# Shifted values copied by engines instead of by DMA, together with a new plan and new buffer counts, in an attention and feed-forward kernel

## The chip, the cores and the metric

The kernel runs on one core of a Trainium2 chip. The metric is the device time in microseconds of one execution. A kernel is executed several times beside the kernel before on the same chip; each execution is called fast or slow, and only fast ones are compared. Of every kernel one execution was also profiled. In the profiles the span (first to last instruction) is 1.7 us shorter than the device time of the same execution (271.4 and 273.11 before), and the last matmul starts 3.0 to 3.1 us before the span ends. That is why the text can speak of "the start of the last matmul" as the end of the work.

## The reference, cut to what matters

Four batches of 768 tokens, 8 heads of 64 features. Three heads use full causal attention, five see 4 sink tokens and a window of 64. The 3072 x 512 result goes through a gated feed-forward layer.

```python
scores = scale * q @ k.T                    # causal; five heads masked to sink + window
a = softmax(scores); x = (a @ v)            # -> 3072 x 512
g = x @ w_gate                              # 512 -> 1536
ffn_out = (gelu(g) * (x @ w_val)) @ w_out   # 1536 -> 512
return x + sigmoid(x @ w_res) * ffn_out
```

## The kernel before

The program is not written in the order in which it runs. It is a graph of tasks (an engine, an assumed duration, the tasks it depends on, a priority, its buffers), and a list scheduler walks through assumed time and fixes each engine's order before anything is compiled. A DMA's assumed landing gets an extra allowance, `late`. `HINTS` overrides priorities by task number. The numbers are guesses that shape the order; on the chip each instruction simply waits for what it depends on, in the order that was fixed.

```python
# inside the scheduler: when a DMA is thought to have landed
st = max(now + dur + 0.8, dma_free[e])
both = min(t.dma, max(0.0, dma_free[other] - st))
dma_free[e] = st + t.dma + both
...                                             # the other queue is pushed back by `both`
t.end = dma_free[e] + 1.6 + t.late
```

The window attention needs the values `va` shifted by half a tile. That shifted copy is `vs`. For the first chunk, tile 1 is copied by VectorE or ScalarE; tiles 2 and 3 go by two DMA transfers from SyncE's queue as long as `VS_DMA` is 1:

```python
for lo, hi, pr in ((1, 2, -75),) + (() if VS_DMA else ((2, 4, 130),)):
    for dst, src, off in ((0, 64, 1), (64, 0, 0)):
        ... e.activation(...) if on == "act" else e.tensor_copy(out=o, in_=i_)   # 64 x (hi-lo)*520
if not VS_DMA:
    return
...                                             # the two transfers, on SyncE:
ts.append(G.add("sp", 1.2, ... e.dma_start(vs[dst:dst + 64, ...], va[src:src + 64, ...])))
```

All weights come through GpSimd's queue, alternately a block of the gate (`wg`) and of the value weights (`wv`), three of each, 512 KB apiece. The attention output of a chunk is normalised, transposed to `xT` and multiplied with these blocks. The first chunk has its `xT` from TensorE, in two halves of 256 columns; for the third chunk half of `xT` comes by a DMA transpose on SyncE's queue:

```python
t = G.add("sp", 1.3, ... e.dma_start(xT[:, cb:cb + 2, :], x16, transpose=True), ..., name="xD")
t.late = 4.0
...
# first chunk: 4 matmuls of 256 columns per weight tile and half
tt = [G.add("pe", ..., xT half deps + [wtok[nm, f // 4]]) for nm, w, dst in (("g", wg, gb), ("v", wv, vb))]
# other chunks and the later part of the first: 512 columns, first cb 0 and 1, then cb 2 and 3
```

While TensorE waits for its first data it runs fillers, 128-column matmuls on a tile of zeros called `blank`; after the weights are there no filler runs.

The softmax here doesn't subtract the row's maximum and nothing guards it: scores larger than these inputs give would overflow.

Of the kernel before, what the change touches and what calls it, by code (L numbers as in the profile page):

```python
# [10 lines left out]
D_MODEL = NHEAD * DHEAD  # L11
# [3 lines left out]
NCB = D_MODEL // 128  # L15
# [3 lines left out]
FP16 = mybir.dt.float16  # L19
FP32 = mybir.dt.float32  # L20
# [23 lines left out]


HINTS = (
    "3:-32.45 398:-150.8 399:-169.97 400:-169.2 401:-150.79 406:481.05 428:533.75 430:564.21 587:-160.89 "
    "608:614.87 617:480.76 622:-210.99 632:614.85 641:12.83 691:-144.85 692:87.22 699:675.15 702:-204.03 "
    "703:-258.78 709:-3118.71 710:-58.5 711:-96.86 715:37.85 723:2455.64 726:495.66 727:-164.98 738:-53.4 "
    "739:-73.39 740:-45.28 746:978.76 747:1556.14 750:37.86 756:509.01 766:947.54 773:2472.11 800:2517.53 "  # L50
    "822:510.02 904:2457.97 910:1055.17 929:2531.59 934:2383.41 959:3505.35 960:1941.27 999:2033.43 "
    "1004:2019.58 1016:3479.78 1061:3558.68 1066:1999 1091:2536 1093:2446.41 1104:4380.53 1107:1523.27 "
    "1109:2000.01 1113:3498.6 1125:4512.49 1136:4434.23 1142:4479.26 1147:4467.42 1152:4500.85 1228:0.01 "
    "1230:3502.12 1236:3515.97 1247:2929.46 1249:3037.51 1258:3472.01 1273:4410.03 1277:0 1278:4479.25 "
    "1304:5410.01 1333:4393.08 1335:5399.49 1338:4000.81 1339:4038.38 1340:4017.53 1347:3851.4 1445:4017.95 "
    "1446:4523.33 1451:3511 1469:6427.61 1479:4849.77 1481:5510 1485:5546.83 1486:6329.91 1490:6560.66 "
    "1501:5520.23 1503:5026.6 1504:5301.09 1539:5026.6 1552:6385.88 1654:4896.34 1675:7440.39 "
)

class Task:  # L60
# [115 lines left out]
SWITCH = 0.1  # L176
SWAP = -3000.0
VK_AT = -18.5
VS_DMA = 1
LAT = {"pe": 0.20, "act": 0.10, "dve": 0.08, "pool": 0.12, "sp": 0.1}  # L180


# [274 lines left out]
def build_kernel(nc, q, k, v, w_gate, w_val, w_out, w_res, out):  # L457
# [3 lines left out]
    many = lambda name, n, shape, dt: [sb(f"{name}{i}", shape, dt) for i in range(n)]  # L461
# [16 lines left out]
    P_er = Pool(many("er", 2, [128, 4608], FP16))  # L478
    P_es = Pool(many("es", 2, [128, 1024], FP16))
    P_ek = Pool(many("ek", 1, [128, 640], FP16))  # L480
    P_x = Pool(many("xtok", 3, [128, 4, D_MODEL], FP32))
    P_x16 = Pool(many("x16", 2, [128, 2, 4, 128], FP16))
    P_xt = Pool(many("xT", 3, [128, NCB, 512], FP16))
    P_h = Pool(many("hT", 2, [128, NF, 512], FP16))
    P_ga = Pool(many("gact", 3, [128, 512], FP16))
    P_sr = Pool(many("srs", 2, [128, 512], FP32))
    P_ot = Pool(many("otile", 3, [128, D_MODEL], FP32))
    P_rc = Pool(many("rcp", 3, [128, 2, 4], FP32))
    psum = nc.alloc_psum_tensor("ps", [128, 8 * 512], FP32)
    one = lambda *bs: [(b,) for b in bs]  # L490
# [6 lines left out]
    def at(buf):  # L497
        if buf.pool is P_ps:
            return psum[:, buf.slot[0] * 512:(buf.slot[-1] + 1) * 512]
        return buf.pool.items[buf.slot]  # L500
# [46 lines left out]
    def dma(eng, prio, cost, out_ap, in_ap, bufs=(), deps=(), name="ld", grp=None):  # L547
        issue = 0.85 if eng == "pool" else 1.2
        return G.add(eng, issue, lambda e: e.dma_start(out_ap(), in_ap), deps, prio, bufs=bufs, dma=cost, name=name, grp=grp)  # L549

    wtok = {}

    def load_weights():
        for j in range(3):
            for nm, t, src in (("g", wg, w_gate), ("v", wv, w_val)):
                s = slice(j * 512, (j + 1) * 512)
                wtok[nm, j] = dma("pool", -20 + j, 2.6, (lambda t=t, s=s: lambda: t[:, :, s])(),
                                  src[:, s].rearrange("(ci p) f -> p ci f", p=128))
        wtok["r"] = dma("pool", -12, 2.6, lambda: wr[:, :, :], w_res.rearrange("(ci p) f -> p ci f", p=128))
        for j in range(4):  # L560
            s = slice(j * 3, (j + 1) * 3)
            wtok["o", j] = dma("pool", -11 + j, 1.95, (lambda s=s: lambda: wo[:, s, :])(),
                               w_out[j * 384:(j + 1) * 384, :].rearrange("(fi p) c -> p fi c", p=128))
            wtok["o", j].late = 2.2

    class B:
        pass
# [12 lines left out]
    def values(b, a, z, base, each, on_engines=False):  # L580
# [23 lines left out]
        if on_engines:  # L604
            ts = []
            for lo, hi, pr in ((1, 2, -75),) + (() if VS_DMA else ((2, 4, 130),)):
                for dst, src, off in ((0, 64, 1), (64, 0, 0)):
# [11 lines left out]
            late_copies.extend(ts)  # L619
            if not VS_DMA:  # L620
                return
# [93 lines left out]
    def ph(c, part):  # L715
        return phase.setdefault((c, part), [])

    def attention(c, segs, xbuf, xtbuf, xtoks, xttoks, l0=0, last=(), ek=None):
# [46 lines left out]
        for P in todo:  # L765
            if P.heads[0] % 2 == 0:
                x16 = Buf(P_x16)
                xdeps = []
            last, tn = weigh(P, tiles, sinks, xbuf, x16, xtoks, xdeps, last, l0)
            if P.heads[0] % 2 == 1:  # L770
                if c >= DT_FIRST and P.p == order[1]:
                    to_features_dma(c, P.heads[0] // 2, P.pr, x16, xdeps, xtbuf, xttoks)
                else:
                  for cb in (P.heads[0] // 2, P.heads[1] // 2):
                    to_features(c, cb, P.pr, x16, xdeps, xtbuf, xttoks, l0, len(tiles))
                if P is todo[-1]:
                    tn.order += [t for _, t in xttoks[-2:]]
                if c == 0 and P is todo[-1]:
                    for t in norms[1:]:
                        t.order.append(xdeps[-1])  # L780
            norms.append(tn)
# [234 lines left out]
    def to_features_dma(c, cb, pr, x16, xdeps, xtbuf, xttoks):  # L1016
        t = G.add("sp", 1.3, lambda e: e.dma_start(
            at(xtbuf)[:, cb:cb + 2, :].rearrange("p c (i k) -> p (c i) k", k=128), at(x16)[:, :, :, :].rearrange("p c i k -> p (c i k)"), transpose=True),
            xdeps, pr - 4003, bufs=[x16, xtbuf], dma=1.2, name="xD")
        t.late = 4.0  # L1020
        ph(c, "xT").append(t)
        xttoks += [(cb, t), (cb + 1, t)]

# [108 lines left out]
    for _ in range(360):  # L1132
# [3 lines left out]
    G.add("act", 0.2, lambda e: e.activation(out=scratch[:, :], in_=blank[:, 0:1], func=AF.Exp), [t_blank], -99,  # L1136
          fset="exp", name="table")
    load_weights()
    for c, segs in enumerate(CHUNKS):
        lt0 = 0  # L1140
# [19 lines left out]
    for c in range(len(CHUNKS)):  # L1160
        gv, gelu = ph(c, "gv"), ph(c, "gelu")
# [23 lines left out]
def bass_duo_attention_split__then__geglu_gated_residual_kernel(  # L1185
    nc: bass.Bass,
    q: bass.AP,
    k: bass.AP,
    v: bass.AP,
    is_retrieval: bass.AP,  # L1190
    n_sink: bass.AP,
    window: bass.AP,
    moe_w_gate: bass.AP,
    moe_w_val: bass.AP,
    moe_w_out: bass.AP,
    moe_w_res: bass.AP,
    out: bass.AP,
):
    assert int(n_sink) == N_SINK and int(window) == WINDOW
    build_kernel(nc, q, k, v, moe_w_gate, moe_w_val, moe_w_out, moe_w_res, out)  # L1200
# [33 lines left out]
```

## Time and profile before

| | before |
|---|---|
| median of the first runs | 273.0 us |
| span of the profiled run | 271.4 us |
| first matmul with weights starts | 20.40 us |
| last matmul starts | 268.33 us |
| TensorE busy | 98% |

Between the two starts lie 247.93 us in which TensorE does almost nothing but follow one matmul with the next. The page's row of shares along the chain of waits says the same: almost all of the end hangs on TensorE itself, and a small part on DMA.

```profile
PE 88%; DMA 6%; DVE 1%; POOL 0%; issue 0%; DVEq 0%
```

In the timelines (start, duration, engine, line, operation; in brackets the idle time before it and what ended that) the last eviction of the first half's `xT` on ScalarE, which frees the weight matmuls, starts at 18.59 and takes 0.38 us, after 0.50 us of idle time.

```profile
8.72 0.64 PE L668 MATMUL ps<-ident,qks 128*64 128x128 f16 x16
...
18.59 0.38 ACT L1033 ACTIVATE xT<-ps 128x256 f16<-128x256 f16 x1 [0.50 <-PE ps L1026]
```

The last `xT` is ready at 18.97, but the value weights land at 20.35: the start is bound by that transfer.

### The profile page before, as it was taken

Reading aid. Unit: us, or ns where it says so; the run is one execution under the profiler, and the core shown is the slowest. Engines: PE = TensorE matmul, PEld = TensorE weight load, DVE = VectorE, ACT = ScalarE, POOL = GpSimd, SP = SyncE. Lnnn points to the kernel's source line nnn. Section 1 sums busy time; section 2 is a strip of 40 time slices with the busy share of each in tenths; the row PEclk is TensorE's granted clock in tenths of the full one; section 3 lists DMA queues with packets and bytes.
Section 4 is the critical chain, followed back from the end, with each engine's and each line's share of the span. In section 5 each row is a group of like instructions: output and inputs, shape, how many; then the busy total and the mean of one; then the engine's idle time right before and its main releaser. Section 6 shows DMA issues by size and latency. Waiting matters only on the chain.

```text
span 271.4 us, 5681 instructions
## 1 busy us (share of the span) xinstructions
PE 265.2 (98%) x2394; PEld 138.8 (51%) x2394; DVE 140.5 (52%) x272; ACT 139.9 (52%) x214; POOL 87.0 (32%) x124
## 2 busy tenths in 40 slices
PE   7989999999999999999999999999999999999995
PEld 7767654455444456344445444455444355444444
DVE  2795354388442567444377354476543457544344
ACT  3784457784435876224764324776332878233210
POOL 8999419995535039990000000000000000000000
PEclk9999999999999999999999999999999999999999
DMA  6999999999999999999954100013100014200013
GB/s 85 172 217 207 188 176 229 173 161 176 189 154 151 154 172 178 179 198 143 139 134 116 42 0 0 2 41 97 61 0 0 0 41 80 77 2 1 0 39 118
DMA packets 97002, 29.13 MB, mean 107 GB/s; under 512 B 85456, under 2 KB 93264, under 8 KB 96976
## 3 DMA queue, kind: packets, MB, share of 16 engines
q0 software_dynamic: 70320, 14.69, 64.7%
q1 hardware_dynamic: 26656, 14.07, 27.1%
q8 instruction: 19, 0.31, 0.5%
q14 instruction: 7, 0.06, 0.1%
HBM read 29.36 MB, written 6.29 MB: 131 GB/s over the span
## 4 chain that ended last, share of the span: by engine, by line
PE 88%; DMA 6%; DVE 1%; POOL 0%; issue 0%; DVEq 0%
PE ps L1072 43%; PE ps L1117 22%; PE ps L1102 7%; PE ps L813 5%; DMA wv<-in_moe_w_val_dram 3%; DMA xT<-x 3%; PE ps L1054 3%; PE ps L947 3%; PE ps L937 2%; PE ps L961 1%; PE ps L1026 1%; PE ps L668 1%; PE ps L904 1%; DVE otile L1124 0%; DVE otile L1121 0%; POOL wg L549 0%
## 5 line engine op out<-in xcount | busy, mean ns | idle before, releaser
L1086 DVE SCALAR_TENSOR_TENSOR hT<-gact,ps 128x512 f16<-128x512 f16 x68 | 45.8, 686 | 67.5 <-ACT gact L1084 38.7
L1084 ACT ACTIVATE gact<-ps 128x512 f16<-128x512 f32 x68 | 40.1, 597 | 74.2 <-PE ps L1072 71.2
L1072 PE MATMUL ps<-xT,wg 128*128 128x512 f16 x272 | 74.7, 379 | 0.6 <-DMA xT<-x 0.6
L1072 PE MATMUL ps<-xT,wv 128*128 128x512 f16 x272 | 74.2, 379 | 0.0
L1117 PE MATMUL ps<-wo,hT 128*128 128x512 f16 (+2 forms) x312 | 70.0, 363 | 0.0
L1072 PEld LDWEIGHTS ps<-xT,wv 128*128 128x128 f16 x272 | 26.3, 98 | 31.8 <-issue 0.7
L1072 PEld LDWEIGHTS ps<-xT,wg 128*128 128x128 f16 x272 | 26.3, 98 | 31.6 <-DMA xT<-x 1.1
L1117 PEld LDWEIGHTS ps<-wo,hT 128*128 128x128 f16 x312 | 27.2, 98 | 26.5 <-issue 0.6
L549 POOL DMA_DIRECT2D qks<-in_k_dram x36 | 28.9, 850 | 31.3 <-DMA qkt<-qks 21.7
L829 ACT ACTIVATE er<-ps 128x1024 f16<-128x1024 f32 (+4 forms) x40 | 34.2, 891 | 9.2 <-PE ps L813 8.8
L549 POOL DMA_DIRECT2D qks<-in_q_dram x36 | 29.2, 863 | 0.8 <-POOLq L1216 0.8
L1102 PE MATMUL ps<-wr,xT 128*128 128x512 f16 x96 | 24.5, 379 | 0.0
L1121 DVE SCALAR_TENSOR_TENSOR otile<-srs,ps 128x512 f32<-128x512 f32 (+2 forms) x26 | 16.7, 643 | 14.6 <-PE ps L1117 12.2
L549 POOL DMA_DIRECT2D va<-in_v_dram x24 | 21.5, 958 | 2.7 <-PE ps L961 2.7
L1105 ACT ACTIVATE srs<-ps 128x512 f32<-128x512 f32 x24 | 14.3, 596 | 12.8 <-PE ps L1102 12.5
L813 PE MATMUL ps<-qkt 64*128 64x64 f16 (+3 forms) x399 | 17.9, 215 | 0.0
L1124 DVE TENSOR_TENSOR otile<-otile,xtok 128x512 f32<-128x512 f32 (+2 forms) x26 | 16.8, 648 | 0.8
L1004 DVE TENSOR_TENSOR xtok<-ps,rcp 128x512 f32<-128x512 f32 (+1 forms) x28 | 17.0, 609 | 0.3
L813 PEld LDWEIGHTS ps<-qkt 64*128 64x128 f16 x399 | 10.3, 94 | 9.2 <-issue 3.8
L1102 PEld LDWEIGHTS ps<-wr,xT 128*128 128x128 f16 x96 | 8.7, 98 | 10.0 <-issue 0.8
L829 ACT ACTIVATE es<-ps 128x1024 f16<-128x1024 f32 (+1 forms) x14 | 12.6, 898 | 1.3 <-PE ps L813 1.1
L1134 PE MATMUL ps<-blank 128*128 128x128 f16 x119 | 11.5, 246 | 1.1 <-DVE blank L521 1.1
(67 smaller groups left out, 208.9 us busy)
## 6 DMA issues: line engine op xcount, KB each, us to landing
out_dram<-otile SPq DMA_DIRECT2D x23, 256.0 KB, 2.0
va<-in_v_dram POOLq DMA_DIRECT2D x24, 128.0 KB, 18.0
qks<-in_k_dram POOLq DMA_DIRECT2D x32, 64.0 KB, 13.7
qks<-in_q_dram POOLq DMA_DIRECT2D x32, 64.0 KB, 13.6
wg<-in_moe_w_gate_dram POOLq DMA_DIRECT2D x3, 512.0 KB, 11.0
wv<-in_moe_w_val_dram POOLq DMA_DIRECT2D x3, 512.0 KB, 11.4
wo<-in_moe_w_out_dram POOLq DMA_DIRECT2D x4, 384.0 KB, 23.5
vs<-va SPq DMA_DIRECT2D x4, 260.0 KB, 5.7
```

The costliest lines, as they stand in the source:

```text
L549: return G.add(eng, issue, lambda e: e.dma_start(out_ap(), in_ap), deps, prio, bufs=bufs, dma=cost, name=name, grp=grp)
L813: return [e.matmul(at(scr)[:, oo:oo + w], lhsT=at(BB.qkt)[half, 1, p, k0:k0 + 128], rhs=at(BB.qkt)[half, 0, p, qq:qq + w], start=True, sto ...
L829: return e.activation(out=o, in_=i_, func=AF.Exp, scale=SM_SCALE)
L1004: t2 = G.add("dve", c_dve(2 * n * 64), lambda e: e.tensor_tensor(out=xview(), in0=avv(0, DHEAD), in1=scale(), op=ALU.mult), [t1] + xdeps, ...
L1072: return lambda e: [e.matmul(at(dst)[:, :], lhsT=w[:, ci, f * 128:(f + 1) * 128], rhs=at(xtbuf)[:, ci, :], start=(ci == 0), stop=(ci == NC ...
L1084: ta = G.add("act", c_act(512), (lambda gb=gb, ga=ga: lambda e: e.activation(out=at(ga)[:, :], in_=at(gb)[:, :], func=AF.Gelu))(), [tg], p ...
L1086: th = G.add("dve", c_dve(512), (lambda vb=vb, ga=ga, f=f: lambda e: e.scalar_tensor_tensor(out=at(h)[:, f, :], in0=at(ga)[:, :], scalar=0 ...
L1102: e.matmul(at(rb)[:, :], lhsT=at(xtbuf)[:, ci, s], rhs=wr[:, ci, :], start=(ci == 0), stop=(ci == NCB - 1))
L1105: ta = G.add("act", c_act(512), (lambda rb=rb, sr=sr: lambda e: e.activation(out=at(sr)[:, :], in_=at(rb)[:, :], func=AF.Tanh, scale=0.5)) ...
L1117: e.matmul(at(fb)[:, w], lhsT=at(h)[:, fi, s], rhs=wo[:, fi, w], start=(fi == 0), stop=(fi == NF - 1))
L1121: t1 = G.add("dve", c_dve(n), (lambda fb=fb, sr=sr, ot=ot, w=w: lambda e: e.scalar_tensor_tensor(out=at(ot)[:, w], in0=at(sr)[:, w], scala ...
L1124: t2 = G.add("dve", c_dve(n), (lambda ot=ot, lt=lt, w=w: lambda e: e.tensor_tensor(out=at(ot)[:, w], in0=at(ot)[:, w], in1=at(xbuf)[:, lt, ...
```

## The change

Its intent: take 0.27 MB of copying off the DMA queues while the weights are loading, let the plan know that one transpose lands later than it thought, and shift buffers from `x` and `xT` to gelu results and output tiles. The priorities were tuned anew for it, so the orders change in many places. `HINTS` is cut here: 24 lines of numbers, all different.

```diff
-    "3:-32.45 398:-150.8 399:-169.97 ... 1675:7440.39 "
+    "0:39.65 1:493.12 14:469.96 398:-242.8 ... ~632:477.39 ~635:510 "
-VS_DMA = 1
+VS_DMA = 0
-    P_x = Pool(many("xtok", 3, [128, 4, D_MODEL], FP32))
+    P_x = Pool(many("xtok", 2, [128, 4, D_MODEL], FP32))
-    P_xt = Pool(many("xT", 3, [128, NCB, 512], FP16))
+    P_xt = Pool(many("xT", 2, [128, NCB, 512], FP16))
-    P_ga = Pool(many("gact", 3, [128, 512], FP16))
+    P_ga = Pool(many("gact", 4, [128, 512], FP16))
-    P_ot = Pool(many("otile", 3, [128, D_MODEL], FP32))
+    P_ot = Pool(many("otile", 5, [128, D_MODEL], FP32))
+        for nm in "gv":
+            wtok[nm, 0].late = 0.7
-        t.late = 4.0
+        t.late = 5.0 if c == 2 else 4.0
```

Line numbers in the profiles after the change are 4 higher (2 higher in the early part).

## The prediction

> **What bounds the kernel now.** I read the page first, for what is full:
>
> ```profile
> PE 265.2 (98%) x2394; PEld 138.8 (51%) x2394; DVE 140.5 (52%) x272; ACT 139.9 (52%) x214; POOL 87.0 (32%) x124
> ```
>
> TensorE is full, and nothing else is. But 98% counts the fillers: 119 of the 2394 matmuls are the warm-up line (`blank`), all before the weights are there. So the time is a start, then one nearly unbroken row of useful matmuls, then a tail. The chain of waits shows what ends the start:
>
> ```profile
> 10.30 0.72 POOL wg L549
> 11.02 9.33 DMA wv<-in_moe_w_val_dram
> 20.35 0.05 issue
> 20.40 1.92 PE ps L1054 x16
> ```
>
> The first block of the value weights lands at 20.35 us, and the feed-forward matmuls begin at 20.40. Next, the waits of TensorE, and the two places in its timeline that belong to them:
>
> ```profile
> PE ps L1054 <- DMA wv<-in_moe_w_val_dram: 1.1, 1, 1.1
> PE ps L1072 <- DMA xT<-x: 0.6, 1, 0.6
> ```
>
> ```profile
> 18.82 0.45 PE L1134 MATMUL ps<-blank 128*128 128x128 f16 x5
> 20.40 0.61 PE L1054 MATMUL ps<-xT,wv 128*128 128x256 f16 x4 [1.12 <-DMA wv<-in_moe_w_val_dram]
> ...
> 109.88 0.59 PE L1072 MATMUL ps<-xT,wg 128*128 128x512 f16 x2
> 111.08 0.39 PE L1072 MATMUL ps<-xT,wg 128*128 128x512 f16 x1 [0.60 <-DMA xT<-x]
> ```
>
> After 20.4 us there is one hole only: two 512-column matmuls start at 109.88 and should be followed 0.43 us later (0.216 us apart, the usual start-to-start distance), the next starts 1.20 us later, so 0.77 us is lost (0.60 counted as idle, because the ends are modelled). The last matmul starts at 268.33, and 3.05 us of evictions and the last store follow. A gain can only come from an earlier start, from that hole, or from fewer drains between matmul shapes.
>
> What sets the landing of the weights I read from the tile views of the weights (one issue each) and of the shifted values:
>
> ```profile
> L549 POOL DMA_DIRECT2D wg<-in_moe_w_gate_dram x1: 777/777/777, 10.3 to 10.3; - x1
> DMA to landing us min/median/max: 6.6/6.6/6.6
> ...
> L549 POOL DMA_DIRECT2D wg<-in_moe_w_gate_dram x1: 770/770/770, 11.8 to 11.8; - x1
> DMA to landing us min/median/max: 11.0/11.0/11.0
> ...
> L549 POOL DMA_DIRECT2D wg<-in_moe_w_gate_dram x1: 750/750/750, 14.6 to 14.6; - x1
> DMA to landing us min/median/max: 13.2/13.2/13.2
> ...
> L628 SPq DMA_DIRECT2D vs<-va x2: 461/499/537, 14.1 to 15.0; - x2
> DMA to landing us min/median/max: 5.9/5.9/6.0
> ```
>
> Issue plus landing time: gate blocks 0, 1, 2 at 16.9, 22.7 and 27.8 us; value block 0 at 20.35 (chain). Steps between landings: 16.9 to 20.35 is 3.5 us, 20.35 to 22.7 is 2.4, and 22.7 to 27.8 holds two transfers, 2.5 each. One step is 1.0 us too long, and it is the one during which the two `vs` transfers (issued at 14.15 and 15.05, landed at 20.1 and 21.0) moved their 0.26 MB. Everything behind is late by that 1.0 us.
>
> **What the Trainium skill says.** "DMA: Bandwidth & Descriptors", Queues, rings and completion order: each DMA engine takes turns between the queues it has work for, packet by packet. The long step agrees: SyncE's queue took its turns from the weights. "TensorE: Matmul & The Clock Gate", Part 3, The mechanism: matmuls are strict FIFO, so one whose weights have not landed holds up all behind it; the hole at 110 agrees. "TensorEngine Tiling (Array Packing)", Key Properties: a change of tiling mode drains TensorE. In the trace a 512-column matmul before another mode takes 0.31 us to the next start instead of 0.216: 0.1 us a switch. "SBUF — State Buffer", Two separate sides: VectorE in a 2-port mode and GpSimd lock each other out. The first chunk's existing engine copies of 64x520 took 0.60 us at 12.04 and 0.29 at 13.15, which fits but does not prove it.
>
> **The change part by part.** From the instruction orders of both kernels:
>
> 1. *Shifted values on engines.* The two early `vs` transfers go; two VectorE copies of 64x1040 come. Queue: minus 1.0 us, so I expect value block 0 at about 19.4, gate block 1 at 21.7, value block 1 at 24.3, gate block 2 at 26.8, and all later weights 1.0 us earlier. VectorE: from 0.29 for 520 columns, 0.55 us each, 1.1 in all, up to 2.4 if both run as the slow one did. VectorE was full there (3.76 of 4.0 us in 10 to 14, 1.93 of 2.0 in 14 to 16), so the first half's normalisations and transposes shift by about 1.1 us. Before, the last of these evictions ended at 18.97 on ScalarE, after a ScalarE idle of 0.5; part of the shift is absorbed. I choose 19.5 for the first weight matmul: mask, window matmuls and eviction end at 19.0 to 19.5.
> 2. *Later landings in the plan.* The new plan puts the second half's first window group (8 of L937 and 2 sink matmuls) ahead of the weights, and asks for the gate block (landed since 16.9) before the value block, which buys 0.43 us (4 x 0.108) until the value block is needed. The useful row after the first weight matmul has 10 small matmuls fewer (0.24 + 0.06 in the chain) and 85 mode switches instead of 88. Summing the row instruction by instruction with the trace's own distances, 247.2 us without the hole becomes 246.7: minus 0.45.
> 3. *But a new wait.* In the old order gate block 2 is first used 105 matmuls after the first weight matmul, in the new one 77 after: 36 of L1054 (4.02), 6 of L1072 (1.30), 8 transposes (0.45), 12 window (0.42), 8 sink (0.35), 7 of L947 (0.21), 6.75 us in all. From 19.5 that is 26.25, and the block lands at 26.8. TensorE waits about 0.55. The end therefore hangs on gate block 2 and not on the first one: any start before 20.07 gives the same end.
> 4. *The hole at 110.* With a landing 1 us later in the plan for that chunk, six more 512-column matmuls stand between the normalisation and the first use of the transposes: 6 x 0.216 = 1.3 us, more than 0.77. Against it: on SyncE a second output store (256 KB) now stands in front of that transpose, and it took 7.7 us to land while the queues were full. I count 0.5 of 0.77 as won.
> 5. *Buffers.* Two instead of three of x and xT, four gelu tiles, five output tiles: TensorE never waits for these buffers in the trace, and two chunks are in flight at most, so 0.
>
> Sum: start 20.40 to 19.5, minus 0.90; gate block 2, plus 0.55; row, minus 0.45; hole, minus 0.50. Total minus 1.3; I add nothing for small new waits on evictions, since two such effects (fewer switches already counted, one more gelu tile) balance. 273.0 - 1.3 = 271.7.
>
> **The rivals.** *The transfers were not what delayed the weights* (a slow generator of descriptors on GpSimd, say). Then landings stay, gate block 2 comes at 27.82, and the row from there gives the last start at 267.8 instead of 268.33: minus 0.5, 272.5. For it: one long step is one observation. Against: the later steps are even. *VectorE becomes the bound of the start*: slow copies, 2.4 us, put the first weight matmul at 20.7 or later; each 0.1 us past 20.07 is 0.1 on the end, so 271.9 to 272.6. *The fewer buffers make a wait*, or the transposes of the third chunk land later still behind the second store: up to 1 us back, 272.5 to 273. *All goes well*: the queue gains 1.3 us (0.26 MB at the 0.2 MB/us of that stretch) and the hole closes fully, 270.9.
>
> **Range and chances.** The middle of these is 271.7, with 272.5 the likeliest miss. Range 270.8 to 272.9. Two per cent would be 5.5 us; the holes after 10 us together are 1.1 + 0.8 plus a few fillers, so faster by 2% is nearly excluded (0.02), and slower by 2% would need a broken stage (0.02); same 0.96.
>
> **What would show it.** Right: no `vs` transfer before 30 us; value block 0 landing near 19.4 and gate block 2 near 26.8; first weight matmul between 19.3 and 20.0, of the gate; a TensorE wait for `wg` of up to 0.6 us near 26; no or a shorter `xT` wait near 109. Wrong: `wv` still landing at 20.3; a TensorE wait for the first half's xT at the start; a wait longer than 0.3 us anywhere after 30 us.

## The result, and the profile after

| | before | after |
|---|---|---|
| median of the runs side by side | 273.0 us (272.31 to 273.31) | 271.74 us (271.4 to 271.96) |
| ratio, 95% interval | | 0.9956 [0.9934, 0.9978] |
| span of the profiled run | 271.4 | 269.8 |
| second load of `q` lands | 8.68 | 9.20 |
| value block 0 lands | 20.35 | 19.64 |
| gate block 2 lands | 27.82 | 26.93 |
| first matmul with weights starts | 20.40 (value) | 20.23 (gate) |
| lost in the hole near 110 us | 0.77 | 0.12 |
| last matmul starts | 268.33 | 266.79 |

A ratio is the mean time of one kernel's fast runs over that of the other's of the same rounds, so it is not quite the ratio of the medians quoted beside it. The class is "same": 0.44% faster, inside 2%.

The page after:

```profile
PE 264.7 (98%) x2392; PEld 138.9 (51%) x2392; DVE 139.2 (52%) x271; ACT 140.7 (52%) x217; POOL 87.1 (32%) x124
...
PE 95%; DMA 2%; DVE 1%; POOL 1%; issue 0%; POOLq 0%; DVEq 0%
```

The busy share of TensorE is unchanged. The share of DMA in the chain fell from 6% to 2%: neither the value weights nor the `xT` of the third chunk are in it any more. What is left is the second load of `q`, from its issue at 3.26 us to its landing at 9.20; from there to 265.7 us the chain names TensorE alone. Of TensorE's waits the longest is now the one for the fillers' own zeros, at the very start, and the list has one other, for that load of `q`. The 0.12 us still lost on `xT` near 110 us is too short for the list.

```profile
PE ps L1138 <- DVE blank L523: 2.0, 1, 2.0
PE ps L672 <- DMA qks<-in_q_dram: 0.3, 1, 0.3
```

The timeline of TensorE shows the new start. Compare it with the lines at 18.82 and 20.40 that the prediction shows.

```profile
9.24 0.64 PE L672 MATMUL ps<-ident,qks 128*64 128x128 f16 x16 [0.27 <-DMA qks<-in_q_dram]
...
19.48 0.27 PE L1138 MATMUL ps<-blank 128*128 128x128 f16 x2
19.68 0.22 PE L941 MATMUL ps<-vs,es 128*64 128x65 f16 x1
...
20.15 0.24 PE L965 MATMUL ps<-vk,ek 128*128 128x65 f16 x2
20.23 0.60 PE L1058 MATMUL ps<-xT,wg 128*128 128x256 f16 x4
```

The gate comes first, and behind the second half's window group (L941, L965), as the orders said. But the fillers do not end at 19.0; they run until 19.5. The timelines of VectorE and ScalarE show the two new copies, and the last `xT` eviction behind them.

```profile
14.55 0.43 DVE L616 COPY vs<-va 64x1040 f16<-64x1040 f16 x1
...
16.76 0.60 DVE L616 COPY vs<-va 64x1040 f16<-64x1040 f16 x1
```

```profile
19.46 0.38 ACT L1037 ACTIVATE xT<-ps 128x256 f16<-128x256 f16 x1
```

The eviction begins at 19.46 instead of 18.59, 0.87 us later; the copies took 1.03 us together, on an engine that was full from 14 to 20 us (busy for 5.81 of 6 us; 5.80 before). It is tempting to put the 0.87 down to the copies, but TensorE's timeline doesn't bear that out. Its transposes of the second load of `q` already start at 9.24 instead of 8.72, 0.52 us late and five microseconds ahead of the first new copy. From there to the start of the last filler (the fillers of a group start 0.056 us apart) TensorE takes 10.29 us, against 10.34 before, with no idle time in the list above. So in this profile the copies delayed TensorE by nothing that can be seen: the start is set by the landing of that load and by TensorE's own fixed row of work and fillers, with the window group at its end. That load lands between 8.27 and 9.68 us in the other fast profiles, in the kernel before and its variants as in the changed one, so the 0.52 us belong to the run and not to the change. The fillers stand where the plan expected TensorE to wait; whether it would start earlier with fewer of them, or would then wait for VectorE, no run tested.

Value block 0 lies ready at 19.64 and nobody waits for it: the bound of the start has moved from the weights' transfer to TensorE's own row.

Gate block 2, by the tile's view (issue, then the time to landing):

```profile
L551 POOL DMA_DIRECT2D wg<-in_moe_w_gate_dram x1: 760/760/760, 14.7 to 14.7; - x1
...
DMA to landing us min/median/max: 12.2/12.2/12.2
```

It lands at 26.93, and its first matmul starts at 27.00, 0.07 us later. In e12, where that matmul did wait, it started 0.05 us after the landing, so there is next to nothing to spare. Near 110 us the timeline of TensorE, and the transpose that it used to wait for:

```profile
110.05 1.03 PE L1076 MATMUL ps<-xT,wv 128*128 128x512 f16 x4
111.03 0.60 PE L1076 MATMUL ps<-xT,wg 128*128 128x512 f16 x2
```

```profile
L1021 SPq DMA_TRANSPOSE xT<-x x1: 2130/2130/2130, 102.1 to 102.1; - x1
...
DMA to landing us min/median/max: 8.9/8.9/8.9
```

Four matmuls at 0.216 us from 110.05 would bring the next to 110.91; it starts at 111.03, so 0.12 us is lost instead of 0.77. The transpose was issued 1.2 us earlier than before (102.14 against 103.36), took 1.2 us longer (8.85 against 7.67), and landed at 110.99 against 111.03. It came no earlier at all. What closed the hole is the six matmuls that the plan put in front of it.

The account of the last matmul's start, 268.33 to 266.79, is 1.54 us: the first weight matmul 0.17 earlier, the hole 0.65 smaller, and 0.72 off the rest of the row, of which 0.18 is a second small hole at 258.4 us that is gone.

### The profile page after: what moved, and what is told of

Its sections match the earlier page's. It is cut to its first block, busy times and chain, and to the rows that moved or that the text cites. A ratio compares the mean times of both kernels' runs of the same rounds, so it can differ in the third digit from the quotient of the medians.

```text
span 269.8 us, 5673 instructions
## 1 busy us (share of the span) xinstructions
PE 264.7 (98%) x2392; PEld 138.9 (51%) x2392; DVE 139.2 (52%) x271; ACT 140.7 (52%) x217; POOL 87.1 (32%) x124
## 4 chain that ended last, share of the span: by engine, by line
PE 95%; DMA 2%; DVE 1%; POOL 1%; issue 0%; POOLq 0%; DVEq 0%
PE ps L1076 44%; PE ps L1121 23%; PE ps L1106 8%; PE ps L817 6%; PE ps L951 3%; PE ps L1058 3%; PE ps L941 2%; DMA qks<-in_q_dram 2%; PE ps L965 2%; PE ps L1138 2%; PE ps L1030 1%; PE ps L672 1%; PE ps L908 1%; POOL qks L551 0%; DVE otile L1128 0%
## 5 line engine op out<-in xcount | busy, mean ns | idle before, releaser
L1076 PE MATMUL ps<-xT,wg 128*128 128x512 f16 x272 | 75.5, 379 | 0.0
L1076 PE MATMUL ps<-xT,wv 128*128 128x512 f16 x272 | 75.4, 379 | 0.0
```

The lines of the kernel that those rows point to most:

```text
L1076: return lambda e: [e.matmul(at(dst)[:, :], lhsT=w[:, ci, f * 128:(f + 1) * 128], rhs=at(xtbuf)[:, ci, :], start=(ci == 0), stop=(ci == NC ...
```

## The experiments

My theory was the prediction's, with one term corrected: taking the transfers away frees the queue by 0.7 to 1.0 us, but VectorE's copies then hold the start; the hole at 110 is closed by the order, which comes from the later landing in the plan; the buffers do nothing. The rivals: the transfers never mattered and the new order alone did it; or the copies cost nothing and something else holds the start; or the hole closes by luck of the landing. The second rival turns out to hold for the first profile of the changed kernel, as shown above. Twelve experiments ran (e1 to e4, e5 to e8, e9 to e12, on two chips). To change one thing without a new plan, several of them let the scheduler finish and then move two tasks in the finished orders; the waits are assigned afterwards as always.

### e1: before without the two transfers, and with nothing in their place

The shifted values of two tiles are set to ones at the very start, so the result is wrong (relative error 12), and all orders stay.

```diff
     span = G.schedule()
+    moved = [t for t in G.order_ if t.name == "vs" and t.eng == "sp"][:2]
+    for t in moved:
+        G.prog["sp"].remove(t); G.order_.remove(t)
+        t.eng, t.deps = "dve", []
+        t.fn = lambda e, dst=dst: e.memset(vs[dst:dst + 64, 1:3, :, :], 1.0)   # ahead of VectorE's other work
```

> The kernel before with every engine's order kept, but the two early transfers of shifted values are dropped; their place in memory is filled with ones early in the run, so the result is wrong on purpose. Theory (the transfers took their turns from the weights): value block 0 lands at 19.4 to 19.7 us instead of 20.35, gate block 2 at 26.8 to 27.0; first weight matmul at about 19.5; hole at 110 stays; span 270.5 against 271.4, time 0.9 us shorter than before. Rival (the weights are paced by GpSimd's issue): landings unchanged, span 271.4.

Measured: value block 0 lands at 19.70 instead of 20.35, gate block 1 at 22.11 instead of 22.74, gate block 2 at 27.19 instead of 27.82. The whole line of weights moves by 0.63 to 0.65 us. The first weight matmul starts at 19.75. TensorE's waits:

```profile
PE ps L1072 <- DMA xT<-x: 0.5, 1, 0.5
PE ps L1054 <- DMA wv<-in_moe_w_val_dram: 0.2, 1, 0.2
```

So the transfers are a cause of the weights' delay, and the start follows the weights if nothing else stands in the way. The size is 0.65 here, not the 1.0 that I read from one long step. The landings of all fast profiles say the same: with the transfers (before, e3, e6, e7) value block 0 lands at 20.32 to 20.74 and gate block 2 at 27.82 to 28.47; without them (the other nine) at 19.36 to 19.88 and 26.93 to 27.56. The medians lie 0.77 and 0.84 us apart. The hole near 110 stays, at 0.67. The time is 272.25 (ratio 0.9992 [0.9972, 1.0013]): a start 0.65 us earlier does not show above the spread of the runs.

### e2: before with the two copies on VectorE

As e1, but the two tasks become copies on VectorE, at the places where the change has them. The result is correct.

```diff
+        t.eng = "dve"
+        t.fn = lambda e, ...: e.tensor_copy(out=vs[dst:dst + 64, 1:3], in_=va[src:src + 64, 2 - off:4 - off])
+        dve.insert(i, t)      # ahead of the second and third normalisation of the first half
```

> The kernel before with TensorE's and ScalarE's order kept; the two early transfers are replaced by two VectorE copies of 64x1040, put where the changed kernel has them. Theory (copies push the first half's attention on VectorE): weights as early as with no traffic (19.4 to 19.7), but the last first-half eviction of the transposes ends about 1 us later than before's 18.97, so the first weight matmul starts at 19.8 to 20.1 and the span is 270.8 to 271.0. Rival (copies are hidden): first weight matmul at 19.5 and span 270.5, as with no traffic.

Measured: value block 0 lands at 19.58, but the first weight matmul starts at 20.60, 0.85 later than in e1 and later than in the kernel before. The copies, and the wait that is new:

```profile
14.29 0.72 DVE L1195 COPY vs<-va 64x1040 f16<-64x1040 f16 x1
...
16.76 0.65 DVE L1195 COPY vs<-va 64x1040 f16<-64x1040 f16 x1
```

```profile
PE ps L937 <- DVE er L865: 0.8, 1, 0.8
```

1.37 us of copies on a full VectorE delay the masks and normalisations behind them, and TensorE waits for a mask (`er`) instead of for the weights. e1 and e2 differ in nothing but the place and kind of these two instructions, and the second load of `q` lands alike (8.37 and 8.27). From its transposes to the last filler TensorE takes 11.66 us here and 10.25 in e1. This shows the rival that the prediction called "VectorE becomes the bound of the start", for the orders of the kernel before. The time is 272.46 (1.0 [0.9985, 1.0015]): this part of the change alone gains nothing. In this profile there is no hole near 110 us although the orders there are those of the kernel before; so its size without the later landing goes down to nothing, too.

### e3: after with the two transfers put back as well

The copies stay; the same two transfers run into a spare tile that nobody reads.

```diff
+    spare = sb("spare", [128, 2, NHEAD, DHEAD + 1], FP16)
+        t = G.add("sp", 1.2, lambda e, ...: e.dma_start(spare[dst:dst + 64, ...], va[src:src + 64, ...]), deps, 0)
+        G.prog["sp"].insert(n_, t)      # first on SyncE, as before
```

> The changed kernel, all orders kept, plus two transfers of the same shape into a spare tile at the time of the old ones. Theory (gate block 2 is the next bound, with almost no slack): gate block 2 lands near 27.9 instead of 26.93, TensorE waits for it about 0.9 us near 27, span 270.6 to 270.8 against 269.8, time near 272.6. Rival (the weights have slack or don't move): no wait, span 269.8.

Measured: value block 0 lands at 20.32 (19.64 after), gate block 2 at 28.47 (26.93). The start is at 21.13, and the wait for gate block 2 appears:

```profile
PE ps L1076 <- DMA wg<-in_moe_w_gate_dram: 0.5, 1, 0.5
```

0.61 us is lost there. The row is the prediction's "new wait": with the traffic it is there, without it the matmul starts 0.07 us after the landing. The start of this run was late because its TensorE clock warmed up late (below, at e5). The better partner for it is therefore e5, which has no traffic, the same start (21.13) and copies that agree to 0.01 us, though it ran on another chip: against e5 the traffic costs 0.96 us on value block 0 (19.36) and 1.48 on gate block 2 (26.99). The time is 272.9 (1.0015 [1.0, 1.003]).

### e4: after with the old landing of the transpose in the plan

```diff
-        t.late = 5.0 if c == 2 else 4.0
+        t.late = 4.0
```

> The changed kernel with the old planned landing (4.0) for the third chunk's transposes; TensorE's order is that of the changed kernel but for 14 matmuls near 107 us. Theory (the six matmuls moved in front closed the hole): a wait of TensorE for xT near 107 us returns, 0.4 to 0.8 us, span 270.3 to 270.6. Rival (the transposes are issued earlier now, or the other buffers closed it): no wait, span 269.8.

Measured, TensorE's waits:

```profile
PE ps L1076 <- DMA xT<-x: 1.6, 1, 1.6
```

The hole is back and larger than it ever was in the kernel before: from 110.09 to 112.10, 1.79 us lost. The transpose was issued at 102.5 and took 9.55 us. With the allowance of 5 us the four profiles of these orders show 0.12 us there (after) or nothing (e3, e5, e12); with 4 us, this. So in these orders the one number in the plan decides whether there is a hole. Its size is not the order's alone: the transpose landed at 112.05 here, 1.06 us later than in the first profile, so I estimate the order's part at 0.7 us (1.79 minus 1.06). The profiled run was also the slowest of the four (273.45; the others 271.95 to 272.58). The median is 272.55 (0.9996 [0.9977, 1.0014]).

### e5: after once more, on another chip

> The changed kernel again, in more rounds, as the yardstick of the next three. Theory: no hole near 107 to 110 in the profile, runs within 271.4 to 272.2 us, a ratio to before of 0.995 to 0.998, and a smaller spread of its runs than before's (272.2 to 274.7 so far), because its transposes' wait is gone. Rival (the gain was chance): ratio 0.999 to 1.001.

Measured: 273.21 (272.27 to 274.5), ratio 0.9991 [0.9955, 1.0027]. The advantage of the first runs does not repeat. The profiled run is the fastest of the six; its landings are as good (value block 0 at 19.36), and there is no hole at 110, but the first weight matmul starts at 21.13, 0.9 later. The copies:

```profile
15.22 0.63 DVE L616 COPY vs<-va 64x1040 f16<-64x1040 f16 x1
...
17.54 0.81 DVE L616 COPY vs<-va 64x1040 f16<-64x1040 f16 x1
```

1.44 us instead of 1.03. Here VectorE does hold TensorE for a while: the chain of waits goes through VectorE, the first new copy included, up to a mask that ends at 16.77 and releases TensorE, and from the transposes of the second load of `q` (9.62) to the last filler TensorE takes 10.82 us instead of 10.29. The other profiles with these orders have 10.81 (e3), 10.70 (e12) and 10.29 (e4). But the first new copy starts 0.7 us later than in the first profile, so something was late before it, and that is TensorE. Its 128-column fillers go from 107 ns to 56 ns apart at some point in the first 8 us. That is what the Trainium skill describes ("TensorE: Matmul & The Clock Gate", Part 1, What's actually happening: a cold clock at half speed until a free-running window of about 3.4 us has been busy, so that the moment varies); the two distances agree with its 107 and 55.8 ns. The last slow filler lies at 5.94 us in the first profile of after, at 5.08 in e4, at 5.50 in e12, and at 7.68 in e3 and e5. Those last two are the runs that start at 21.13; the others start between 20.06 and 20.43. The change also moved the zeros of the fillers behind other memsets, so the first filler starts at 2.02 instead of 1.06. The kernels with 1.06 were warm by 3.8 to 7.05 us, those with 2.02 by 5.08 to 7.68. Two late starts in the five fast profiles with these orders (after, e3, e4, e5, e12) are not enough to call the shift of that memset the cause; that a late clock goes with a late start is seen in both.

### e6: before with the later landing of the transpose, alone

```diff
-        t.late = 4.0
+        t.late = 5.0 if c == 2 else 4.0
```

> The kernel before with the later planned landing of the third chunk's transposes alone; TensorE's order is before's up to the 1190th matmul. Theory (this one line closes the hole, and the hole's size varies from run to run): first weight matmul still at 20.4, no wait for xT near 110, span 270.5 to 270.8, time 0.5 to 0.8 us under before. Rival (the hole moves elsewhere): a wait of 0.3 us or more after 100 us, span 271.2 or more.

Measured:

```profile
PE ps L1072 <- DMA xT<-x: 0.8, 1, 0.8
```

The hole did not close in the profiled run (0.93 us lost), which was the slowest of six (273.94; the others 272.75 to 273.13). The transpose took 9.17 us. With the old priorities the allowance of 1 us is not enough for a landing that late. The time is 272.98 (0.9983 [0.9954, 1.0011]).

### e7: e6, and the first blocks' landings as in the change

```diff
+        for nm in "gv":
+            wtok[nm, 0].late = 0.7
```

> As the last, and the first weight blocks planned 0.7 us later, which in this order only swaps the first gate and value groups (4 matmuls each): the transfers of shifted values stay. Theory: the gate block landed long ago, so the first weight matmul starts at 19.9 and the value group right at its landing, 20.35: 0.45 us won, span 270.1 to 270.3. If the span equals the changed kernel's 269.8 within 0.4, the engine copies are not needed for its gain. Rival (first-half transposes are not ready at 19.9): start at 20.3, span as the last.

With the old priorities this addition swaps gate and value. TensorE's timeline:

```profile
19.50 0.60 PE L1056 MATMUL ps<-xT,wg 128*128 128x256 f16 x4
20.39 0.83 PE L1056 MATMUL ps<-xT,wv 128*128 128x256 f16 x6 [0.28 <-DMA wv<-in_moe_w_val_dram]
```

The gate starts at 19.50, and the value matmuls start at 20.39, where the kernel before starts them. The fourth gate matmul starts at 19.83 and the next should follow 0.11 later, so 0.45 us is lost between. Four matmuls, 0.43 us, are done earlier. That is the size that the prediction gave to this swap. The hole near 110 is 0.19 here. The time is 272.9 (0.9977 [0.9948, 1.0006]). In the changed kernel itself the 0.7 does nothing: built without it, TensorE's order is the same to the last instruction. There the swap comes from the new priorities.

### e8: e7, with the two copies on VectorE after the first half

```diff
+    at_ = norms_[4]            # after the first half's normalisations
+        dve.insert(dve.index(at_), t)
```

> As the last, and the two transfers of shifted values replaced by two VectorE copies that stand behind all of the first half's attention on VectorE (it idled from 20.4 to 22.8 in the kernel before). Theory (traffic costs 0.65 to 1.0, and copies cost only where VectorE is full): value block 0 at 19.4 to 19.7, first weight matmul of the gate at 19.3 to 19.5, no wait at gate block 2 (it is used 105 matmuls later), span 269.4 to 269.7, which is 0.1 to 0.4 below the changed kernel. Rival (the window matmuls now wait for the copies, near 21.3): a wait of 0.3 us or more there, span 269.8 or more.

Measured: the first weight matmul at 20.09, but the second half's window matmuls now wait for the copies. TensorE's and VectorE's timelines:

```profile
22.71 0.22 PE L939 MATMUL ps<-vs,es 128*64 128x65 f16 x1 [0.71 <-DVE vs L1194]
```

```profile
21.02 1.63 DVE L1194 COPY vs<-va 64x1040 f16<-64x1040 f16 x2
```

The two took 1.63 us here. The wait has moved, not gone. The time is 272.37 over eight runs (0.9951 [0.9922, 0.998]); the profiled run is the slowest of them (273.44), so the wait of 0.7 is not the usual case either. Its median is lower than that of the changed kernel (273.21).

### e9: after a third time

> The changed kernel a third time, as yardstick on whatever chip this is. Theory (its start hangs on VectorE[...] and on the first loads' landing): first weight matmul between 20.2 and 21.2, no hole near 110, span 269.8 to 270.7, ratio to before 0.995 to 0.999.

Measured: five runs between 271.66 and 274.39, ratio 0.9987 [0.9952, 1.0023], and one, the profiled one, of 687.01 us. It is in no comparison. Two lines of its page:

```profile
PE 680.6 (99%) x2392; PEld 249.2 (36%) x2392; DVE 142.8 (21%) x271; ACT 144.3 (21%) x217; POOL 86.9 (13%) x124
...
L1076 PE MATMUL ps<-xT,wg 128*128 128x512 f16 x272 | 187.7, 836 | 0.0
```

All other engines are busy for as long as ever (DVE 139.2 to 142.8 us); TensorE alone was slow throughout, while the mean granted clock of the run is given as 1.0. The distances have a pattern: 512-column matmuls start 0.62 or 0.48 to 0.49 us apart instead of 0.216, fillers 187 ns and now and then 56 ns. 187 is 56 plus 131 ns, and 0.216 plus two or three times 0.133 gives 0.48 and 0.62. It looks like a full clock with pauses of 0.13 us put in, not like half a clock; that is a reading of the distances, no more. Nothing in the kernel differs from e5, and why this execution went so is not explained here.

All 15 fast runs of the changed kernel fall into two groups: ten between 271.4 and 272.6 and five between 273.7 and 274.5. No profile fell into the second, so its cause stays open. The gap between the groups is not firm: e12, with the same orders, has a run of 273.02 us, and the kernel before spreads from 272.24 to 274.9 on the same chip.

### e10: e7, with one copy on ScalarE and one on VectorE

```diff
+        on = "act" if t.seq == 404 else "dve"
+        at_ = ph(0, "table")[0] if on == "act" else cands[4]   # ScalarE: ahead of the gelu table's load
+        G.prog[on].insert(G.prog[on].index(at_), t)
```

> The kernel before's order with the later planned transposes and the gate block first, as before; of the two copies one stands on ScalarE ahead of its table load, the other on VectorE behind the second half's first mask. Theory: no copy stands in the first half's chain, so the first weight matmul starts at 19.4 to 20.1; both copies end by 21.9, the wait for them of 0.98 us seen before shrinks to 0.3 or less; a hole of 0 to 0.8 us near 110 may remain; span 269.5 to 270.7, faster than the changed kernel by 0 to 1 us. Rival (ScalarE's copy delays the first gelu): a wait of TensorE for PSUM near 22 to 24 us.

Measured: the first weight matmul starts at 19.32, no wait near 110, and one wait that is new:

```profile
PE ps L1056 <- ACT gact L1060: 0.4, 1, 0.4
```

ScalarE's copy takes 1.07 us and sits ahead of the table load and the first gelu; TensorE's next weight matmul starts 0.60 us after the small one before it, and the profile counts 0.4 of that as a wait for the gelu. The time is 272.23 (272.02 to 272.46), ratio 0.9963 [0.9941, 0.9984].

### e11: e10, with the transpose ahead of the store and the shifted values on SyncE

```diff
+    xd = [t for t in ph(2, "xT") if t.dma][0]
+    sp.remove(xd); sp.insert(k, xd)      # k: right behind the last transpose of q and k before it
```

> As the last, and on SyncE's queue the third chunk's transposes stand ahead of the output store and the two transfers of shifted values that preceded them. Theory (in-order issue and the 0.5 MB ahead delay them): issued at 101 instead of 102.6, landed by 110 instead of 112; no hole near 110 in the profile, and a smaller spread of the runs (under 1.0 us). Rival (the loads on the other queue alone set the landing): it still lands at 111 or later and the hole stays.

Measured, by the view of `xT`:

```profile
L1019 SPq DMA_TRANSPOSE xT<-x x1: 1231/1231/1231, 100.5 to 100.5; - x1
...
DMA to landing us min/median/max: 6.0/6.0/6.0
```

It lands at 106.51, 4.5 us earlier than before, and nothing waits for it. In e10, behind the store and the `vs` transfers, it took 8.2 us; what stands in front of it on SyncE's queue is worth 2 us of its landing between these two profiles. The wait for the gelu is there as in e10. The time is 272.07 (271.77 to 272.35), ratio 0.9956 [0.9934, 0.9977]. The five fast runs of the changed kernel have a median of 272.42 and spread over 2.7 us; these six spread over 0.6. It beats the kernel before, and has the lower mean of the two (0.9956 against 0.9987 of the same before, with intervals that overlap).

### e12: after with three output tiles and three xT again

```diff
-    P_xt = Pool(many("xT", 2, [128, NCB, 512], FP16))
+    P_xt = Pool(many("xT", 3, [128, NCB, 512], FP16))
-    P_ot = Pool(many("otile", 5, [128, D_MODEL], FP32))
+    P_ot = Pool(many("otile", 3, [128, D_MODEL], FP32))
```

> The changed kernel with three output tiles and three buffers of the transposes, as before the change; the order on every engine is unchanged, only the waits for free buffers differ. Theory (buffers do nothing): the same time as the changed kernel in this call, within the intervals. Rival (the output tiles give VectorE room): 0.3 us or more slower.

The orders come out the same on every engine. The profiled span is 269.7 us against 269.8, the time 272.4 (271.47 to 274.17; 0.9982 [0.995, 1.0014]). These buffers make no difference that the runs can show. This run shows one more thing, because its first weight matmul starts at 20.06, just inside the prediction's limit of 20.07:

```profile
26.40 1.27 PE L1076 MATMUL ps<-xT,wg 128*128 128x512 f16 x4
```

The group of four takes 1.27 us instead of the 1.03 that four take at the usual distance; between its second and third start lie 0.45 us. Gate block 2 lands at 27.02 here, and 0.24 us is lost waiting for it.

## Why the prediction was right or wrong

The total was right, 271.7 predicted and 271.74 measured in the runs beside which it was made, and so was the class. That it fits to 0.04 us is luck, since the same kernel's later medians are 273.21 and 272.42. The terms under it were not all right; two errors cancelled. Of the signs that it named, the landings (19.64 and 26.93), the gate first, and no long wait after 30 us came; a first weight matmul between 19.3 and 20.0 and a wait for `wg` did not.

- *The queue.* Right in its mechanism: e1 takes the traffic away and all weights land 0.63 to 0.65 us earlier, e3 puts it back and they are late. The term was mis-sized: 1.0 from one long step of 3.5 against 2.5 us, while the same step takes 2.54 to 2.88 in the nine profiles without the transfers. Measured 0.65 (e1), 0.71 and 0.89 (after, value block 0 and gate block 2), about 0.8 between the medians, and more, 0.96 and 1.48, only in e3 against e5.
- *The start*, "20.40 to 19.5, minus 0.90". This step failed: it moved by 0.17. The prediction looked for the bound on VectorE, wrote that "part of the shift is absorbed" on the way to the last eviction and chose 19.5. In the profile TensorE itself was the bound: its fixed row takes 10.99 us from the transposes of the second load of `q` to the first weight matmul, of which the window group that the new order puts ahead is 0.55 (19.68 to 20.23). Begun at 8.72 as before, it would have ended at 19.71 (an estimate, if VectorE had kept up); it began at 9.24, because that load landed 0.52 us later in this run. The rival "VectorE becomes the bound of the start" is real, but not seen in this profile: e2 against e1 shows it in the old orders (20.60 against 19.75), and in e3, e5 and e12 the same row is 0.4 to 0.5 us longer, with waits for VectorE in it.
- *The new wait*, "gate block 2, plus 0.55". It did not appear in the result, because the start was late enough: 26.93 minus the 6.75 us of the row is 20.18, so a start before that would have gained the end nothing. That it exists is shown by e12 (start 20.06, 0.24 lost) and e3 (0.61 lost). The step "any start before 20.07 gives the same end" therefore holds about where it said. This is why the total survived: with minus 0.90 and plus 0.55 the prediction had minus 0.35 for start and wait together; minus 0.17 came.
- *The row*, "minus 0.45". Measured 0.72, of which 0.18 is a hole at 258.4 that the prediction left out; the rest, 0.54, is the term.
- *The hole*, "minus 0.50" of 0.77. Measured minus 0.65. The mechanism is shown from both sides, in direction: e4 brings the hole back with one number, and in after the transpose lands no earlier while the hole is gone. Its size is not a constant: 0.77, 0.67 and 0 in the three profiles with the orders of before (before, e1, e2), 1.79 in e4, and with the later landing on the old priorities 0.93, 0.19, 0.38 and twice none (e6, e7, e8, e10, e11). The transpose behind the second store took longer (8.85 against 7.67 us), as the prediction feared, and its earlier issue paid for that; but 9.2 us in e6, with a single store in front, shows that the landing alone can vary by as much.
- *Buffers*, 0. Right for `xT` and the output tiles (e12: equal orders, equal span). Three gelu tiles could not be planned with the new priorities, so that one was not tried alone.
- *Two sums among the rivals* are off. By the prediction's own terms, transfers that did not matter give a last start of 268.04 (27.82 - 6.75 + 246.7 + 0.27), thus 272.7 and not 272.5, because the 0.27 left of the hole was forgotten; and "all goes well" gives about 271.1, not 270.9.

The sum from the profiles is minus 0.17, minus 0.65, minus 0.72, thus minus 1.54 us, against minus 1.30 predicted. What the prediction did not foresee is that the gain would be smaller than the spread from run to run: in the two later calls the changed kernel was only 0.1% ahead, inside the interval. How much of the 1.26 us of the first comparison is the kernel's and how much that session's stays open; I would call it 0.1 to 0.4%. Where the queue's earlier weights went is settled only for single profiles: in the old orders VectorE's copies pay them back (e2); in the changed kernel they keep away the wait for gate block 2 that its own order would bring (e3), and the start itself gains only 0.17 us, because TensorE's own row, begun late, reaches the first weight matmul no sooner. How much the copies cost the changed kernel on average stays open: 0 in two of its profiles (after, e4) and 0.4 to 0.5 us, other waits included, in three.

## What to carry to other kernels

Moving a copy from a queue to an engine can move the wait (e2) if that engine is full in the same stretch; look at its share in the few microseconds that end in the critical landing, not over the span. A landing that the plan gets wrong by 1 us costs a hole in a full engine, and putting the transfer further ahead in its queue (e11) made it land 4.5 us earlier, where six matmuls in front of its use (6 x 0.216 us) give 1.3. Before a late start is put down to a change, look for the first instruction at which the two traces part: here it lay five microseconds ahead of the copies. When a change is worth 0.5%, one comparison on one chip cannot tell it: repeat it on another before keeping it.

## What the Trainium skill lacked or had wrong

- "TensorE: Matmul & The Clock Gate", Part 1, gives a window of 3.4 us and half a microsecond of variation for the clock's warm-up. With fillers from 1.06 us on, the last slow one lay between 3.8 and 7.05 us, from 2.02 on between 5.08 and 7.68: 2.7 to 6.0 us after the first filler, a far wider variation. Idle time does not explain the late ones: in e3 and e5, 5.7 us after the first filler, the list of waits has none in between.
- The same page warns that the clock can be stuck at a low step for over 50 us. One execution here (e9) was slow from the first filler to the last matmul, 685.3 us, with mostly 0.62 us per 512-column matmul instead of 0.216, while the granted clock was reported as 1.0. The page says neither that a whole run can go so, nor that the distances can look like pauses of 0.13 us at full clock.
- "DMA: Bandwidth & Descriptors", Queues, rings and completion order, gives the turns between queues but no price. Here 0.27 MB on SyncE's queue delayed 512 KB blocks on GpSimd's by 0.65 us (e1), about 0.8 between the medians of all fast profiles. A transpose of the same size took from 6.0 (e11) to 9.5 us (e4) to land; with the same four transfers just in front of it, 8.85 (after) and 9.55 (e4).
- "TensorEngine Tiling (Array Packing)", Key Properties, names the drain at a change of mode without a size: 0.1 us here (0.31 instead of 0.216 to the next start).
- "SBUF — State Buffer", Two separate sides, describes the lock between VectorE and GpSimd. It does not say what a DMA's issue on GpSimd costs a copy. Equal copies on VectorE took 0.29 to 0.60 us (64x520) and 0.43 to 0.87 us (64x1040) in the fast profiles. Every 64x520 copy above 0.42 us, and every 64x1040 copy, ran beside a DMA issue on GpSimd; those beside none took 0.29 to 0.41. That fits the lock; no run here proved it, since none took GpSimd's work away.
